# A long convolution and two split-precision MLPs on one core: the inverse transform of two tiles in one go, two PSUM buffers for `ob`, weight conversions every seven pairs, the last unit in halves

## The chip, the cores and the metric

One core of one Trainium2 chip runs the program. The metric is the device time of one execution in microseconds (us).

## The reference

```python
def _attn_ref(x, v, pos_emb, w1, w2):            # x, v: 1 x 12480 x 128
    h_filt = (np.maximum(pos_emb @ w1, 0) @ w2) * np.exp(-0.01 * np.arange(S))[:, None]
    u = x * v
    y = irfft(rfft(u, 2 * S) * rfft(h_filt, 2 * S))[:S]      # along the sequence
    return x * y
def _moe_ref(x, w_in, w_out):                    # 128 -> 2048 -> 128
    r = np.maximum(x @ w_in, 0); return (r * r) @ w_out
def _moe2_ref(x, w_in, w_out):
    h = x @ w_in; return (h / (1 + np.exp(-1.702 * h))) @ w_out
# result = _moe2_ref(_moe_ref(_attn_ref(...)))
```

The weights of the two MLPs are float64 in the reference's inputs, the rest is float32.

## The kernel before, in words

**Convolution.** The sequence is folded into N1 = 99 by N2 = 127, and the transform is done in two stages of matmuls in fp32. The stage `stage_s2` (from about 88 to 226 us) works through NP = 50 pairs of frequencies. In step p of its loop TensorE does `spectra(p)` (into `xk`), in odd steps also `features` (into `fk`), in every fourth step two `filters` (into `hk`), and then `back(p - 2)` (into `ob`). VectorE does `product(p - 1)` (four products `t` in one instruction, L374, and a difference into `P`, L378), GpSimd does the matching sum (L377), and ScalarE copies `fk`, `hk` and `ob` out of PSUM. `ob` goes to `A` (L390) and from there to the DRAM buffer `bd`. In PSUM `xk` and `hk` have two buffers each, `fk` one and `ob` one (pool `obp`).

**Weights.** The float64 weights are read as pairs of 32-bit words. `conversion` makes of each chunk a high and a low part in fp32r, in nine instructions: eight on VectorE (L149, L151, L155, L157, L158, L160, L165, L169) and a copy on ScalarE (L167). An object `Weights` starts chunks by a table (start, gap, lead); each `tick` lets every running conversion issue its next instruction. The eight chunks of the first MLP start at steps 3, 9, 15, ... of `stage_s2`, one tick for each pair; `work.finish` issues what is left before the MLP. The four chunks of the second MLP start at units 6, 18, 30 and 42 of the MLP loop.

**MLP loop.** The 12480 positions are cut into 25 tiles of 490 to 502 columns. A unit is a pair of 128-wide blocks of the 2048 hidden features of one tile: `unit_in` does six matmuls of about 500 columns into `hin` (three for each block: high times high, low times high, high times low), ScalarE and VectorE make `gh` and `gl` of it (`gate`, `high`, `low`), and `unit_out` does six matmuls into `acc`, LAG = 4 units later. Eight units make a tile. The first 40 units are all of the first MLP (layer 0); from then on units of both layers alternate. When tile `t`'s layer 0 is done, `split` makes the input of its layer 1.

**Inverse transform.** The convolution's last step lies inside that loop. `load_b` brings pieces of `bd` into `uv`, `combine_two` adds and subtracts them on VectorE into `b` (three homes, two of them in the old tile `Gs`), and `front_y(t + 1)` in unit j = 3 of tile t (4 from t = 5 on) does the inverse of one tile in TensorE: 5 segments with 4 small matmuls each (99x64 weights, 98 or 99 columns, fp32) into `yps`, which has two buffers in the pool `pms`. VectorE multiplies `yps` with x into `y` (L566), and `front_x` splits `y`. Two segments at the sequence's end are done by `front_rest` in unit j = 1 of tile 1, copied into `yr` (L587) and given out to the tiles from 2 on. Ahead of the loop the inverse of tile 0 stands between dummy matmuls (`spare`).

**Order.** Every engine runs its instructions in the order in which the code is written (`manual_schedule`). An instruction of an engine that waits holds up all that stand behind it there.

Of the kernel before, what the change touches and what calls it, by code (L numbers as in the profile page):

```python
# [23 lines left out]
N1, N2 = 99, 127  # L24
# [48 lines left out]
def widths():  # L73
# [25 lines left out]
def conv_mlp_kernel(ctx: ExitStack, tc: tile.TileContext, xc, xt, vc, pt, w1, w2,  # L99
# [76 lines left out]
    class Weights:  # L176
# [145 lines left out]
    def stage_s2(sp, mp, A, w2b, hooks, work):  # L322
# [3 lines left out]
        obp = tc.tile_pool(name="obp", bufs=1, space=PSUM, reuse_waits="tile")  # L326
# [5 lines left out]
        with kp as kp, obp as obp:  # L332
            def features(g):
# [5 lines left out]
                ps = kp.tile([128, FK, 128], FP32, tag="fk", name="fk", bufs=1)  # L339
# [98 lines left out]
    b_t, x_t, pending = {}, {}, []  # L438
# [29 lines left out]
    def pend(k):  # L468
        pending.extend((k, op) for op in (ALU.add, ALU.subtract))

    def combine_next(n):
        for i in range(min(n, len(pending))):
            combine_two(*pending.pop(0))

    def load_b(bp, t):


        last = max(p[0] for p in whole(t)) // JG
        for k in range(loaded[0], last + 1):
            uv = bp.tile([N1, 2, JG, 2, D], FP32, tag="uv", name="uv", bufs=2)  # L480
            for h in range(2):
                nc.sync.dma_start(out=uv[:, h], in_=bd[h, k * JG:(k + 1) * JG].rearrange("j k c d -> k j c d"))
            b = sums(bp, k % 3)
            b_t[k] = uv, b
            pend(k)
        loaded[0] = last + 1
# [23 lines left out]
    def mlp(lp, bp, work):  # L510
# [44 lines left out]

        def front_y(t):


            ps = pms.tile([D, 512], FP32, tag="m", name="yps")
            inverse(ps, whole(t))  # L560
            if t == 0:
                return split_first(ps, x_t.pop(0)[:, 0:width(0)])
# [9 lines left out]
        def load_rest():  # L572


            k = REST[0][0] // JG
            assert all(p[0] // JG == k for p in REST)
# [315 lines left out]
```

## Time and profile before

| | us |
|---|---|
| median of 3 runs (1381.61 to 1383.54) | 1382.43 |
| the profiled execution | 1382.61 |
| span of its instructions | 1380.8 |
| TensorE busy (matmuls) | 1372.9 (99%) |
| VectorE busy | 1109.2 (80%) |
| ScalarE busy | 948.9 (69%) |
| GpSimd busy | 61.0 (4%) |

The span runs from the first instruction to the last. The profiled execution is 1.8 us longer than its span. In a row of a timeline the first number is the start and the second the length, both in us; PE is TensorE's matmul stream, PEld its weight loads, DVE VectorE, ACT ScalarE. A matmul's recorded length overlaps that of the next, so the step from one start to the next tells what it takes of TensorE. An fp32 matmul stands in the trace as two records with a load each, and an fp32r matmul as one.

### The profile page before, as it was taken

Reading aid. Unit: us, or ns where it says so; the run is one execution under the profiler, and the core shown is the slowest. Engines: PE = TensorE matmul, PEld = TensorE weight load, DVE = VectorE, ACT = ScalarE, POOL = GpSimd, SP = SyncE. Lnnn points to the kernel's source line nnn. Section 1 sums busy time; section 2 is a strip of 40 time slices with the busy share of each in tenths; the row PEclk is TensorE's granted clock in tenths of the full one; section 3 lists DMA queues with packets and bytes.
Section 4 is the critical chain, followed back from the end, with each engine's and each line's share of the span. In section 5 each row is a group of like instructions: output and inputs, shape, how many; then the busy total and the mean of one; then the engine's idle time right before and its main releaser. Section 6 shows DMA issues by size and latency. Waiting matters only on the chain.

```text
span 1380.8 us, 19037 instructions
## 1 busy us (share of the span) xinstructions
PE 1372.9 (99%) x7754; PEld 1139.9 (83%) x7754; DVE 1109.2 (80%) x1224; ACT 948.9 (69%) x1066; POOL 61.0 (4%) x61
## 2 busy tenths in 40 slices
PE   9999999999999999999999999999999999999998
PEld 8888886888888888888888888888888888888887
DVE  7559998888887787778777887778777887778887
ACT  2655554888776777667767777777777777777776
POOL 3013332000000000000000000000000000000000
PEclk9999999999999999999999999999999999999999
DMA  9968875111210000000000100001000000000000
GB/s 257 306 214 271 270 263 190 55 48 61 70 39 20 15 21 27 20 28 20 27 20 8 40 27 20 8 28 39 20 15 20 28 19 8 9 8 8 9 15 15
DMA packets 45843, 89.25 MB, mean 65 GB/s; under 512 B 4135, under 2 KB 30556, under 8 KB 44988
## 3 DMA queue, kind: packets, MB, share of 16 engines
q1 hardware_dynamic: 36744, 63.33, 15.4%
q10 hardware_dynamic: 9012, 24.70, 4.7%
q8 instruction: 61, 1.00, 0.3%
q14 instruction: 26, 0.21, 0.0%
HBM read 63.21 MB, written 24.81 MB: 64 GB/s over the span
## 4 chain that ended last, share of the span: by engine, by line
PE 92%; DVE 6%; issue 1%; ACT 1%; DMA 1%; SPq 0%; DVEq 0%; ACTq 0%
PE acc L595 13%; PE acc L596 13%; PE acc L597 13%; PE hin L595 13%; PE hin L596 13%; PE hin L597 13%; PE s L295 5%; PE yps L553 3%; DVE t L374 2%; PE ob L388 2%; PE xk L365 2%; PE hk L357 1%; PE fk L342 1%; DVE r L278 1%; DVE words L151 0%
## 5 line engine op out<-in xcount | busy, mean ns | idle before, releaser
L647 DVE TENSOR_TENSOR gl<-g,gh 128x1004 fp32r<-128x1004 f32 (+4 forms) x400 | 477.1, 1193 | 36.9 <-ACT gh L643 36.8
L623 ACT ACTIVATE g<-hin 128x1004 f32<-128x1004 f32 (+4 forms) x200 | 201.0, 1005 | 225.3 <-PE hin L597 219.2
L595 PE MATMUL acc<-gh,w 128*128 128x502 f32 (+4 forms) x800 | 313.8, 392 | 0.6 <-DVE lo L530 0.6
L596 PE MATMUL acc<-gl,w 128*128 128x502 f32 (+4 forms) x800 | 311.4, 389 | 0.6 <-DVE gl L647 0.6
L597 PE MATMUL acc<-gh,w 128*128 128x502 f32 (+4 forms) x800 | 311.4, 389 | 0.0
L595 PE MATMUL hin<-hi,w 128*128 128x502 f32 (+4 forms) x798 | 310.3, 389 | 0.3 <-ACT g L623 0.3
L596 PE MATMUL hin<-lo,w 128*128 128x502 f32 (+4 forms) x798 | 310.5, 389 | 0.0
L597 PE MATMUL hin<-hi,w 128*128 128x502 f32 (+4 forms) x798 | 309.4, 388 | 0.0
L638 DVE TENSOR_TENSOR g<-hin,g 128x1004 f32<-128x1004 f32 (+4 forms) x200 | 238.7, 1194 | 45.7 <-ACT g L628 45.5
L628 ACT ACTIVATE g<-hin 128x1004 f32<-128x1004 f32 (+4 forms) x200 | 200.1, 1000 | 70.4 <-PE hin L597 62.4
L636 DVE CAST gh<-g 128x1004 fp32r<-128x1004 f32 (+4 forms) x185 | 125.8, 680 | 137.1 <-ACT g L624 137.0
L624 ACT ACTIVATE g<-g 128x1004 f32<-128x1004 f32 (+4 forms) x200 | 208.0, 1040 | 6.3
L643 ACT CAST gh<-g 128x1004 fp32r<-128x1004 f32 (+4 forms) x200 | 202.7, 1013 | 0.3 <-DVE g L638 0.3
L595 PEld LDWEIGHTS acc<-gh,w 128*128 128x128 f32 x800 | 150.5, 188 | 33.9 <-DVE lo L530 1.0
L595 PEld LDWEIGHTS hin<-hi,w 128*128 128x128 f32 x798 | 150.2, 188 | 34.1 <-ACT g L623 3.5
L596 PEld LDWEIGHTS acc<-gl,w 128*128 128x128 f32 x800 | 150.9, 189 | 30.4 <-DVE gl L647 1.4
L597 PEld LDWEIGHTS acc<-gh,w 128*128 128x128 f32 x800 | 150.5, 188 | 30.4
L597 PEld LDWEIGHTS hin<-hi,w 128*128 128x128 f32 x798 | 150.4, 188 | 30.4
L596 PEld LDWEIGHTS hin<-lo,w 128*128 128x128 f32 x798 | 150.3, 188 | 30.2
L374 DVE TENSOR_TENSOR t<-xk,hc 128x1024 f32<-128x1024 f32 (+1 forms) x50 | 60.1, 1202 | 11.6 <-ACT hc L359 11.6
L377 POOL TENSOR_TENSOR P<-t 128x256 f32<-128x256 f32 (+1 forms) x50 | 48.4, 968 | 155.4 <-DVE t L374 141.0
L388 PE MATMUL ob<-P,m 128*128 128x256 f32 x198 | 53.0, 391 | 0.3 <-issue 0.3
(79 smaller groups left out, 954.2 us busy)
## 6 DMA issues: line engine op xcount, KB each, us to landing
m<-in_c_s_dram SPq DMA_DIRECT2D x49, 256.0 KB
bd<-A ACTq DMA_DIRECT2D x24, 512.0 KB
uv<-bd SPq DMA_DIRECT2D x62, 198.0 KB
x<-in_xc_dram SPq DMA_DIRECT2D x16, 384.0 KB
v<-in_vc_dram SPq DMA_DIRECT2D x16, 384.0 KB
Gs<-gd ACTq DMA_DIRECT2D x10, 512.0 KB
gd<-G SPq DMA_DIRECT2D x3, 1344.0 KB
pos<-in_pt_dram SPq DMA_DIRECT2D x16, 198.0 KB
```

The lines of the kernel that those rows point to most:

```text
L374: nc.vector.tensor_tensor(out=t[:, 0:n], in0=xk[:, 0:n].unsqueeze(3).to_broadcast(full), in1=hc.unsqueeze(2).to_broadcast(full), op=ALU.mult)
L388: nc.tensor.matmul(out=ob[:, j], lhsT=m[:, j, 1, :], rhs=P[:, j])
L595: nc.tensor.matmul(out=out, lhsT=a, rhs=hl[0], start=first, stop=False)
L596: nc.tensor.matmul(out=out, lhsT=a, rhs=hl[1], start=False, stop=False)
L597: nc.tensor.matmul(out=out, lhsT=b, rhs=hl[0], start=False, stop=last)
L623: nc.scalar.activation(out=g, in_=ps, func=ACTF.Relu)
L624: nc.scalar.activation(out=g, in_=g, func=ACTF.Square)
L628: nc.scalar.activation(out=g, in_=ps, func=ACTF.Sigmoid, scale=1.702)
L636: nc.vector.tensor_copy(out=gh, in_=g)
L638: nc.vector.tensor_tensor(out=g, in0=ps, in1=g, op=ALU.mult)
L643: nc.scalar.copy(out=gh, in_=g)
L647: nc.vector.tensor_tensor(out=gl, in0=g, in1=gh.bitcast(FP32), op=ALU.subtract)
```

## The change

The kernel after does these things otherwise:

- `ob` and `fk` share one tag with two PSUM buffers, and the pool `obp` is gone.
- The first MLP's conversions start at steps 3, 10, 17, ... of `stage_s2` (gap 7 in place of 6, fetched 7 steps ahead). The eighth chunk does not start there, and the end of the seventh is left too; both are issued in the first seven units of the MLP loop, one or two ticks a unit (`rest.go_on`). The second MLP's chunks start at units 10, 21, 32 and 43.
- `front_ps` does the inverse of tiles t + 1 and t + 2 one behind the other, in even tiles t alone. `front_rest` stands in the same place of tile 2, ahead of the two. The first such place is unit 2. The products with x follow in that unit and the next (`front_y`).
- The pieces of `bd` come by a queue (`queue_for`, `load_next`, `combine_next`): at most two are loaded and not yet summed, and a sum is issued two or more steps of the loop behind its load. The four sums for tiles 1 and 2 stand ahead of the loop.
- In the last unit each 128-wide block has a PSUM tile, a sigmoid, a product, a cast and a difference of its own, and the last output is copied and sent in two halves of 245 columns, by two queues.

```diff
@@ widths
-        if t > 1 and left:
-            n = min(left, -(-RESTW // (NTILE - 2)))
+        if t > 2 and left:
+            n = min(left, -(-RESTW // (NTILE - 3)))
@@ Weights
-        def finish(self, n=1 << 30):
-            while n and (self.run or self.plan):
-                self.tick(1 << 30)
-                n -= 1
+        def go_on(self, n, at=0):
+            for i in range(n):
+                self.tick(at)
@@ stage_s2
-        obp = tc.tile_pool(name="obp", bufs=1, space=PSUM, reuse_waits="tile")
-                ps = kp.tile([128, FK, 128], FP32, tag="fk", name="fk", bufs=1)
+                ps = kp.tile([128, FK, 128], FP32, tag="fk", name="fk")
-                ob = (kp.tile([128, FK, D], FP32, tag="fk", name="ob", bufs=1).rearrange(
-                    "p (k c) d -> p k c d", c=2) if p == NP - 2 else
-                      obp.tile([128, 2, 2, D], FP32, tag="ob", name="ob"))
+                ob = kp.tile([128, FK, D], FP32, tag="fk", name="ob").rearrange("p (k c) d -> p k c d", c=2)
@@ loads and sums of the inverse
+    def load_sum(bp, k, n):
+        b_t[k] = load_uv(bp, k), home_of.pop(k)() if k in home_of else sums(bp, k % 3)
+        pending.extend((n, k, op) for op in (ALU.add, ALU.subtract))
+    def combine_next(n, most=1):
+        for i in range(most):
+            if pending and pending[0][0] <= n:
+                combine_two(*pending.pop(0)[1:])
+    def load_next(bp, n):
+        if queue and len({k for _, k, _ in pending}) < 2:
+            load_sum(bp, queue.pop(0), n + 2)
@@ the inverse
+        def front_ps(t):
+            ps_t[t] = pms.tile([D, 512], FP32, tag="m", name="yps")
+            inverse(ps_t[t], whole(t))
         def front_y(t):
-            ps = pms.tile([D, 512], FP32, tag="m", name="yps")
-            inverse(ps, whole(t))
+            ps = ps_t.pop(t)
@@ the last unit and the last output
+            if (l, t, j) == seq[-1]:
+                ps = ps[:, 0, 0:n], pms.tile([128, 512], FP32, tag="m", name="hin")[:, 0:n]
+            if (l, t, j) == seq[-1]:
+                for c in range(2):
+                    nc.scalar.activation(out=g[:, c], in_=ps[c], func=ACTF.Sigmoid, scale=1.702)
+            elif (l, t, j) == seq[-1]:
+                for c in range(2):
+                    nc.vector.tensor_tensor(out=g[:, c], in0=ps[c], in1=g[:, c], op=ALU.mult)
+                    cut = w // 2 if t == NTILE - 1 else w
+                    for a, b, queue in ((0, cut, nc.sync if cut < w else nc.scalar), (cut, w, nc.scalar)):
+                        if a < b:
+                            nc.scalar.copy(out=o[:, a:b], in_=acc[1][:, a:b])
+                            queue.dma_start(out=out[:, STARTS[t] + a:STARTS[t] + b], in_=o[:, a:b])
@@ ahead of the loop
-        front_y(0)
+        front_first()
-        work.finish()
+        queue_for(1)
+        queue_for(2)
+        load_next(bp, -2)
+        load_next(bp, -2)
+        load_x(lp, 1)
+        load_x(lp, 2)
+        combine_next(0, 4)
-        work = Weights([(2, 0), (3, 0), (2, 1), (3, 1)], 6, 12, 4)
+        rest, work = work, Weights([(2, 0), (3, 0), (2, 1), (3, 1)], 10, 10.67, 3)
@@ the loop
+            rest.go_on(1 if n < 2 else 2, 1 << 30)
-                    if t == 1 and j == 1:
-                        front_rest()
-                    if j == 3 + late and t + 1 < NTILE:
-                        front_y(t + 1)
+                    at = 3 + (t >= SHIFT // PAIRS) if t else 2
+                    lead = t % 2 == 0 and t + 2 < NTILE
+                    if lead and j == at:
+                        if t == 2:
+                            front_rest()
+                        front_ps(t + 1)
+                        front_ps(t + 2)
+                        front_y(t + 1)
+                    elif lead and j == at + 1:
+                        front_y(t + 2)
+                    load_next(bp, n)
@@ the call of stage_s2
-            work = Weights([(i, c) for c in range(NWC) for i in range(2)], 3, 6, 5)
+            work = Weights([(i, c) for c in range(NWC) for i in range(2)], 3, 7, 7)
-            work.finish(EARLY)
+            work.go_on(EARLY)
```

The change moves instructions at three places that matter below. The first is TensorE at the start of the MLP loop, where `hin` is a unit's first matmuls, `yps` an inverse and `acc` a unit's second matmuls. Before, from the fourth unit's last matmuls on, the inverse of tile 1 alone stands ahead of the first `acc`:

```order
L595 MATMUL hin<-hi_2304,w_958 128x492
L596 MATMUL hin<-lo_2305,w_958 128x492
L597 MATMUL hin<-hi_2304,w_958 128x492
L553 MATMUL yps<-ci_61,Gs 64x99 x8
L553 MATMUL yps<-ci_61,b 64x99 x4
L553 MATMUL yps<-ci_61,b 64x98 x4
L553 MATMUL yps<-ci_61,b 64x99 x4
L595 MATMUL acc<-gh,w_958 128x492
```

After, the inverse of tiles 1 and 2 stands behind the third unit, ahead of the fourth:

```order
L558 MATMUL yps<-ci_61,Gs 64x99 x8
L558 MATMUL yps<-ci_61,b 64x99 x4
L558 MATMUL yps<-ci_61,b 64x98 x4
L558 MATMUL yps<-ci_61,b 64x99 x4
L558 MATMUL yps<-ci_61,b 64x98 x4
L558 MATMUL yps<-ci_61,Gs 64x99 x4
L558 MATMUL yps<-ci_61,Gs 64x98 x4
L558 MATMUL yps<-ci_61,Gs 64x99 x4
L558 MATMUL yps<-ci_61,Gs 64x98 x4
L600 MATMUL hin<-hi_2291,w_958 128x492
```

So 40 small matmuls in place of 20 stand there, one unit earlier.

The second place is VectorE at the same time: `lo` is the last of tile 0's input, `uv` what the sums read, `gh` and `gl` the first unit's results. Before, a unit's work comes ahead of the sums:

```order
L543 TENSOR_TENSOR lo_2305<-y,hi_2304 128x492
L169 TENSOR_TENSOR w_958<-words,w_958 128x512
L636 CAST gh<-g 128x2x492
L647 TENSOR_TENSOR gl<-g,gh 128x2x492
L464 TENSOR_TENSOR b<-uv 99x2x256
L466 TENSOR_TENSOR b<-uv 99x2x2x128
```

After, four sums come first, and instructions of two conversions lie between the units':

```order
L548 TENSOR_TENSOR lo_2292<-y,hi_2291 128x492
L460 TENSOR_TENSOR b<-uv 99x2x256
L462 TENSOR_TENSOR b<-uv 99x2x2x128
L460 TENSOR_TENSOR Gs<-uv 99x2x256
L462 TENSOR_TENSOR Gs<-uv 99x2x2x128
L149 TENSOR_SCALAR words<-words 128x512
L653 CAST gh<-g 128x2x492
L169 TENSOR_TENSOR w_958<-words,w_958 128x512
L151 SCALAR_TENSOR_TENSOR words<-words 128x512
L669 TENSOR_TENSOR gl<-g,gh 128x2x492
```

The sums moved ahead of everything of the loop, and the eighth conversion moved in from `stage_s2`.

The third place is unit j = 3 of tile 2. Before, TensorE has the inverse of tile 3 there, and VectorE's row at that time ends in the product of tile 3 with x:

```order
L151 SCALAR_TENSOR_TENSOR words<-words 128x1024
L530 TENSOR_TENSOR lo_2792<-acc,hi_2791 128x494
L636 CAST gh<-g 128x1004
L647 TENSOR_TENSOR gl<-g,gh 128x1004
L566 TENSOR_TENSOR y<-yps,xs 128x493
```

After, TensorE has the rest's eight matmuls and the inverse of tiles 3 and 4, in three tiles of a pool with two buffers, so that the third takes the buffer of the rest:

```order
L558 MATMUL yps<-ci_61,words 64x98 x8
L558 MATMUL yps<-ci_61,Gs 64x99 x4
L558 MATMUL yps<-ci_61,Gs 64x98 x4
L558 MATMUL yps<-ci_61,Gs 64x99 x4
L558 MATMUL yps<-ci_61,Gs 64x98 x4
L558 MATMUL yps<-ci_61,b 64x99 x4
L558 MATMUL yps<-ci_61,b 64x98 x4
L558 MATMUL yps<-ci_61,b 64x99 x4
```

and VectorE, at the same time, has the rest's copy into `yr` where the product of tile 3 stood:

```order
L169 TENSOR_TENSOR w_2239<-words,w_2239 128x1024
L535 TENSOR_TENSOR lo_2782<-acc,hi_2781 128x494
L653 CAST gh<-g 128x2x492
L669 TENSOR_TENSOR gl<-g,gh 128x2x492
L592 COPY yr<-yps 128x196
L579 TENSOR_TENSOR y<-yps,xs 128x493
```

The second row with `b` in TensorE's piece is where tile 4 begins; its first matmul waits for VectorE.

## Rows read from the trace of the kernel before

**Rows 1.** The page, part 1: busy us (share) xinstructions of each engine.

```profile
PE 1372.9 (99%) x7754; PEld 1139.9 (83%) x7754; DVE 1109.2 (80%) x1224; ACT 948.9 (69%) x1066; POOL 61.0 (4%) x61
```

**Rows 2.** Waits from 88 to 227 us: us in total, times, longest.

```profile
PEld ob L388 <- issue: 3.4, 13, 0.7
PEld xk L365 <- DVE t L374: 2.8, 9, 0.6
```

**Rows 3.** Timeline, weight loads of `stage_s2`: start, length, instruction, idle before it.

```profile
100.23 1.86 PEld L357 LDWEIGHTS hk<-w2b,fs 64*128 64x128 f32 x32 [0.33 <-issue]
...
155.65 1.86 PEld L357 LDWEIGHTS hk<-w2b,fs 64*128 64x128 f32 x32 [0.33 <-issue]
...
162.08 0.73 PEld L388 LDWEIGHTS ob<-P,m 128*128 128x128 f32 x4 [0.23 <-issue]
...
166.62 1.86 PEld L357 LDWEIGHTS hk<-w2b,fs 64*128 64x128 f32 x32 [0.33 <-issue]
...
211.56 1.86 PEld L357 LDWEIGHTS hk<-w2b,fs 64*128 64x128 f32 x32 [0.33 <-issue]
```

**Rows 4.** Timeline, VectorE in `stage_s2` and at its end.

```profile
199.29 1.22 DVE L165 SCALAR_TENSOR_TENSOR words<-words 128x512 f32<-128x512 f32 x1
...
216.22 1.22 DVE L165 SCALAR_TENSOR_TENSOR words<-words 128x512 f32<-128x512 f32 x1
...
219.36 1.22 DVE L374 TENSOR_TENSOR t<-xk,hc 128x1024 f32<-128x1024 f32 x1
...
221.03 1.22 DVE L374 TENSOR_TENSOR t<-xk,hc 128x1024 f32<-128x1024 f32 x1
```

**Rows 5.** The tile `yps`: idle time of the loader before its loads (us, times).

```profile
  issue: 8.8, 25
```

**Rows 6.** Timeline, TensorE around the inverse of tile 6.

```profile
376.58 0.39 PE L597 MATMUL hin<-hi,w 128*128 128x502 f32 x1
376.90 0.56 PE L553 MATMUL yps<-ci,Gs 99*64 99x98 f32 x8
377.29 1.53 PE L553 MATMUL yps<-ci,b 99*64 99x99 f32 x32
378.75 0.49 PE L595 MATMUL acc<-gh,w 128*128 128x492 f32 x1
379.07 0.39 PE L596 MATMUL acc<-gl,w 128*128 128x492 f32 x1
```

**Rows 7.** Timeline, start of the MLP loop.

```profile
236.31 0.67 DVE L543 TENSOR_TENSOR lo<-y,hi 128x492 fp32r<-128x492 f32 x1
...
240.06 0.38 PE L597 MATMUL hin<-hi,w 128*128 128x492 f32 x1
240.77 0.49 PE L595 MATMUL hin<-hi,w 128*128 128x492 f32 x1 [0.33 <-ACT g L623]
...
244.20 0.49 PE L595 MATMUL acc<-gh,w 128*128 128x492 f32 x1
```

**Rows 8.** Timeline: the rest's copy, and tile 3's inverse and product.

```profile
264.24 0.35 DVE L587 COPY yr<-yps 128x196 f32<-128x196 f32 x1
...
290.71 0.48 PE L553 MATMUL yps<-ci,Gs 99*64 99x99 f32 x6
...
295.56 0.66 DVE L566 TENSOR_TENSOR y<-yps,xs 128x493 f32<-128x493 f32 x1
```

**Rows 9.** Windows: length, busy us of PE, PEld, DVE, ACT, POOL; PEclk; DMA; GB/s.

```profile
266.00:290.00 24.00, 24.00 (x139) 19.71 (x138) 20.15 (x25) 20.73 (x23) 0.00 (x0) 1.00 0.26 83
...
1379.00:1380.80 1.80, 0.00 (x0) 0.00 (x0) 0.00 (x0) 0.00 (x0) 0.00 (x0) 0.59 0.13 47
```

**Rows 10.** Timeline, TensorE where the layers begin to alternate.

```profile
365.87 0.49 PE L595 MATMUL acc<-gh,w 128*128 128x492 f32 x1 [0.61 <-DVE lo L530]
```

**Rows 11.** Timeline, the end.

```profile
1374.40 0.49 PE L596 MATMUL acc<-gl,w 128*128 128x490 f32 x1 [0.56 <-DVE gl L647]
...
1377.13 0.57 ACT L666 COPY o<-acc 128x490 f32<-128x490 f32 x1 [2.83 <-PE acc L597]
```

More of the change, by code (lines that the diff above doesn't have):

```diff
@@ L330, in pair @@
             return min(2, N1 - 2 * p)
-        with kp as kp, obp as obp:
+        with kp as kp:
             def features(g):
@@ L466, in combine_two, with load_uv, queue_for @@
             nc.vector.tensor_tensor(out=b[:, :, 0:4:3], in0=u, in1=v[:, :, ::-1], op=op)
[L468 to L475, printed above, removed]
-        last = max(p[0] for p in whole(t)) // JG
[L479 to L486, printed above, removed]
+    def load_uv(bp, k):
+        uv = bp.tile([N1, 2, JG, 2, D], FP32, tag="uv", name="uv", bufs=2)
+        for h in range(2):
+            nc.sync.dma_start(out=uv[:, h], in_=bd[h, k * JG:(k + 1) * JG].rearrange("j k c d -> k j c d"))
+        return uv
+    def load_sum(bp, k, n):
+        b_t[k] = load_uv(bp, k), home_of.pop(k)() if k in home_of else sums(bp, k % 3)
+        pending.extend((n, k, op) for op in (ALU.add, ALU.subtract))
+    def queue_for(t):
+        last = max(p[0] for p in whole(t)) // JG
+        queue.extend(range(loaded[0], last + 1))
+        loaded[0] = max(loaded[0], last + 1)
+    def combine_next(n, most=1):
[5 more added lines that the diff above has]
+            load_sum(bp, queue.pop(0), n + 2)
     late_h = []
@@ L570, in front_y, with rest_home @@
             y_t[t] = y
-        def load_rest():
-            k = REST[0][0] // JG
-            assert all(p[0] // JG == k for p in REST)
-            uv = bp.tile([N1, 2, JG, 2, D], FP32, tag="uv", name="uv", bufs=2)
-            for h in range(2):
-                nc.sync.dma_start(out=uv[:, h], in_=bd[h, k * JG:(k + 1) * JG].rearrange("j k c d -> k j c d"))
-            b = words(6, 2)[0:N1].bitcast(FP32).rearrange("p (j s c d) -> p j s c d", j=JG, s=2, c=2)
-            b_t[k] = uv, b
-            pend(k)
+        def rest_home():
+            return words(6, 2)[0:N1].bitcast(FP32).rearrange("p (j s c d) -> p j s c d", j=JG, s=2, c=2)
         def front_rest():
@@ L636, in gate @@
                 nc.vector.tensor_copy(out=gh, in_=g)
+            elif (l, t, j) == seq[-1]:
+                for c in range(2):
+                    nc.vector.tensor_tensor(out=g[:, c], in0=ps[c], in1=g[:, c], op=ALU.mult)
             else:
@@ L642, in high @@
             if l == 1:
-                nc.scalar.copy(out=gh, in_=g)
+                for c in halves((l, t, j)):
+                    nc.scalar.copy(out=gh[:, c], in_=g[:, c])
         def low(un):
             key, ps, g, gh, gl = un
-            nc.vector.tensor_tensor(out=gl, in0=g, in1=gh.bitcast(FP32), op=ALU.subtract)
+            for c in halves(key):
+                nc.vector.tensor_tensor(out=gl[:, c], in0=g[:, c], in1=gh.bitcast(FP32)[:, c], op=ALU.subtract)
             g_t[key] = (gh, gl)
@@ L664, in unit_out @@
                 else:
[L665 to L667 removed]
+                    o = tp.tile([D, MW], FP32, tag="o", name="o")
+                    w = width(t)
+                    cut = w // 2 if t == NTILE - 1 else w
[3 more added lines that the diff above has]
+                            queue.dma_start(out=out[:, STARTS[t] + a:STARTS[t] + b], in_=o[:, a:b])
         seq = []
@@ L683, in mlp @@
         spare(7)
-        front_y(0)
+        front_first()
         spare(1)
-        work.finish()
+        assert all(p[0] // JG == REST[0][0] // JG for p in REST)
+        home_of[REST[0][0] // JG] = rest_home
+        queue_for(1)
[5 more added lines that the diff above has]
+        combine_next(0, 4)
         prev = None
-        work = Weights([(2, 0), (3, 0), (2, 1), (3, 1)], 6, 12, 4)
+        rest, work = work, Weights([(2, 0), (3, 0), (2, 1), (3, 1)], 10, 10.67, 3)
         for n in range(len(seq) + LAG):
+            rest.go_on(1 if n < 2 else 2, 1 << 30)
             work.tick(n)
+            assert n < 7 or not rest.run and not rest.plan
             if n >= LAG:
```

45 lines of the change are left out of this document (24 added, 21 removed).

## The prediction

> **What bounds the kernel now.** I began with the page's busy shares: TensorE is busy for 1372.9 us of a span of 1380.8 [rows 1], so nothing that merely frees another engine can move the time; only TensorE's own small losses can. Then I looked for those losses. The list of waits over `stage_s2` names two: before `ob` the loader stood 3.4 us in 13 places, and before `xk` it waited 2.8 us in 9 places for VectorE's product `t` [rows 2]. The tile view of the inverse names a third: 25 times the loader sat idle before `yps`, 8.8 us in all, 0.35 us each [rows 5]. Since recorded matmuls overlap, I read the true price of such a place from the steps between starts [rows 6]. The timelines of the loop's start [rows 7], of the turn to alternating layers [rows 10] and of the end [rows 11] show one wait each. Together that is some 14 us that a change could reach, about 1% of the time. The rest of TensorE's time is matmuls back to back, which the change leaves in number and nearly in shape.
>
> **Part 1, two buffers for `ob` and conversions every seven pairs.** A period of four pairs ends with `hk`. An undisturbed one lasts 166.62 - 155.65 = 10.97 us and has one wait of 0.23 us before `ob` in it, at 162.08, where `ob` stands one step behind the previous `ob` and must wait for ScalarE to empty the one buffer [rows 3]. With two buffers shared with `fk`, that `ob` takes the buffer of a `fk` that was copied well before, so a period of pure work is 10.97 - 0.23 = 10.74 us. The ten periods from 100.23 to 211.56 took 111.33 us [rows 3], against 107.4 of pure work: 3.9 us are there to be won. But VectorE was the second limit, and it must allow that. Six pairs and one conversion take 216.22 - 199.29 = 16.93 us on it, and a bare pair 221.03 - 219.36 = 1.67 us [rows 4], so a conversion is 16.93 - 6 x 1.67 = 6.91 us. Before, that is 2.82 us a pair, more than TensorE's 10.74 / 4 = 2.69; this is where the waits for `t` come from. After, it is (7 x 1.67 + 6.91) / 7 = 2.66 us a pair, just under 2.69. TensorE becomes the bound, with 1% to spare. The spare is thin and the work is uneven: with a gap of seven, two conversion instructions fall into one pair of every seven, so that VectorE falls behind for a step. I leave 0.7 us of the waits for `t` in, and take 3.2 us off. At the stage's end the same wait for `ob` delays the last pairs; the chain there runs on through the copy, `bd` and the first inverse, and I take 0.3 us more. Part 1: **-3.5 us**, bounds -4.4 (all waits gone, and 0.5 at the end) and -1.5 (VectorE keeps most of its waits). The conversion that leaves the stage goes to the MLP's first units, where VectorE's row has it between the units' work; its cover there is the four units that lie between a unit's first and second matmuls.
>
> **Part 2, the inverse of two tiles in one go.** From 376.58 to 379.07 TensorE goes from a long matmul over one inverse to the second long matmul behind it: 2.49 us [rows 6]. Two long steps in their own place cost 2 x 0.23 = 0.46. The small records are 0.0415 us apart: the last of the 32 starts at 377.29 + 1.53 - 0.25 = 378.57, so (378.57 - 377.29) / 31. Forty of them are 1.70 with their slower first ones. What is left, 2.49 - 0.46 - 1.70 = 0.33 us, is paid for each change of shape, out and back, whatever stands between. There are 25 such places [rows 5]: 24 tiles and the rest. After, 12 are left. Part 2: 13 x 0.33 = **-4.3 us**, bounds -3.9 and -4.5.
>
> **Part 3, a new wait in tile 2.** There the rest and two tiles take three tiles of PSUM from a pool with two buffers. Tile 4's inverse takes the buffer of the rest, so it waits until VectorE has copied the rest into `yr`. VectorE's row there is the same as before up to that copy, with L169 in place of L151, one long conversion instruction for another. Before, its next instruction at this point, the product, began at 295.56, and the inverse had begun at 290.71 [rows 8]. The copy takes 0.35 [rows 8], so the buffer is free at 295.91, or 5.2 us after the inverse's start. TensorE has the rest's 16 records and tile 3's 40 to do until then, 56 x 0.043 = 2.4 us. It then stands for 5.2 - 2.4 = **+2.8 us**, and behind it in TensorE's row stand `acc` and all the rest of the program, so nothing hides it. Bounds: +2.0, if ScalarE and VectorE take up the unit without delay, and +3.4, if ScalarE is still busy with the unit before it.
>
> **Part 4, the loop's start.** Before, the fourth unit's matmuls waited for ScalarE to empty `hin`: the step from 240.06 to 240.77 is 0.71 where 0.23 is usual [rows 7]. After, two inverses fill that hole: **-0.5 us**. The cover needs four sums to be ready. They stand directly behind `lo`, which ends at 236.98 [rows 7]; at 0.6 each, about the step of `lo`-sized instructions, they would end near 239.4, and the inverse could start at 240.4. Their last one is needed only half way through, near 242. If the transfers of `uv` come 2.6 us later than I think, the gain is gone, and each us more costs one. Bounds -0.6 and +1.0.
>
> **Part 5, the rest.** Where layers begin to alternate, `acc` waited 0.61 us for `lo`, held up by a long conversion instruction [rows 10]. After, a short one stands there, but also a sum, and tile 5's inverse no longer gives VectorE a rest: -0.2 us, bounds -0.5 and +0.5. At the end TensorE waited 0.56 us for the last `gl` but one [rows 11]; with the sigmoid and the product in halves that begins about 0.3 us earlier. Of the 0.57 us of the last copy [rows 11], half comes ahead of the first transfer, which may save 0.2. Together **-0.5**, bounds -0.8 and -0.1. The waits that stand on SyncE's queue (the loads of x and `uv` for two tiles) are issued a tile ahead of their use; I cost them at nothing, covered by those 16 units.
>
> **Sum.** -3.5 - 4.3 + 2.8 - 0.5 - 0.2 - 0.5 = -6.2 us. The profiled execution took 1382.6, its span and 1.8 around it, and stands 0.2 above the median of the runs, 1382.43, which is less than I can resolve. Summed against 1382.6 that gives **1376.4 us**.
>
> **Rivals.**
>
> *A. The clock falls in the new wait.* At the end of the program, when TensorE has done nothing since the last `acc`, the granted clock of the last 1.8 us is 0.59 on average [rows 9], so it falls from 2.4 to 1.2 GHz after an idle stretch. The new wait of 2.8 us is longer than any other that TensorE has inside the loop. If the clock falls there, TensorE works at half speed until it is granted again; no row prices that, and 6 us at half speed, 3 us lost, is my choice between 0 and 10. Time 1379.4. Against it: the wait is not as long as the idle stretch at the end, and dense work stands on both sides. The Trainium skill, "TensorE: Matmul & The Clock Gate", section "HAM oscillation — how this bites in real kernels", tells that waits between groups of matmuls send the engine back to the lower clock, each anew. By that rule this case would be likelier than I put it; the trace of before has no such wait within the loop to show it.
>
> *B. VectorE keeps `stage_s2`.* With 2.66 us against 2.69 a pair there is hardly any room, and GpSimd works at the same time. If VectorE stays the bound at uneven pairs, part 1 gives 1.5 and the time is 1378.4.
>
> *C. The new wait isn't there or is short,* because VectorE gets to the copy earlier or the wait takes the place of one that would come behind it. The time is 1373.6. For it: units behind a long break find everything ready. Against it: before, TensorE shows no waits in that stretch to be saved.
>
> *D. Slower: the first layer runs out of cover.* For the first 40 units ScalarE and VectorE do nearly as much as TensorE: 20.73 and 20.15 us in 24.0 [rows 9], of which one inverse gave TensorE's partners 2.0 us of rest in every tile. In odd tiles that rest is gone, and 20.73 of 22.0 us is 94%. If the chain through ScalarE, VectorE and back gets longer than the four units' lag, every unit waits. It decides from 22.0 us of ScalarE's work in a tile on, 1.3 us more than now. To end above 1385.2 it would have to cost 9 us over four tiles, 0.28 us in each of 32 units; then 1386. Against it: before, ScalarE is idle at the end of each tile, and no `acc` waits there.
>
> **How the numbers follow.** Forecast 0.53, A 0.17, B 0.12, C 0.12, D 0.06. The range takes in B and A on one side and C on the other: 1373.5 to 1380.2. A measurement of this kernel tells about 0.2% or 2.8 us from no change, so faster means under 1379.7. The forecast, C, B and nearly half of A lie there: 0.83. The other half of A and what lies between forecast and D: 0.12. D alone makes it slower: 0.05.
>
> **What would show it.** In the trace after: no idle before `ob` in steps with an even pair, and periods of `hk` of 10.74 to 10.85 us; 12 places with idle time before `yps` in place of 25 beside tile 0's; one wait of TensorE for `yr` of 2 to 3.4 us near 290; no idle between the third and fourth unit; a first wait for `gl` at the end under 0.4 us. The forecast is wrong if the clock after 290 us is under 1.00, if the waits before `xk` stay at nearly 3 us, if TensorE waits for sums at unit 2, or if `acc` waits for `gl` in tiles 1 to 4.

## The result, and the profile after

The changed kernel takes 1389.62 us (median of four runs, 1389.27 to 1390.99), the kernel before 1382.02 beside it: a ratio of 1.0055, 95% interval 1.0037 to 1.0072. It is slower by about 7.6 us. I had forecast 1376.4 us and a range up to 1380.2.

The page's busy shares of the changed kernel say no more than those of before [rows 1] did: TensorE has 1.2 us less work in a span that is 7.2 us longer.

```profile
PE 1371.7 (99%) x7754; PEld 1143.2 (82%) x7754; DVE 1108.6 (80%) x1226; ACT 948.4 (68%) x1069; POOL 61.0 (4%) x61
```

So the time lies in waits. The list of TensorE's waits (engine, tile, line, what it waited for: us in total, times, longest) is the view that tells it:

```profile
PE yps L558 <- DVE yr L592: 3.2, 1, 3.2
PE acc L602 <- DVE w L169: 2.6, 1, 2.6
PE acc L601 <- DVE gl L669: 1.7, 3, 1.0
...
PE hin L600 <- ACT g L636: 0.9, 1, 0.9
PE acc L600 <- DVE lo L535: 0.7, 1, 0.7
```

The first was forecast. The second, the fourth and most of the third were not. To see where they stand in time, I read from the timeline when the first `hk`, the first `yps` and the first `acc` matmul of certain units start (a8 is unit 8's), and when the last instruction ends. The lengths between these points, in us, for the profiled execution of each kernel that was run:

| kernel | to first hk | to first yps | to a0 | to a8 | to a28 | to a56 | to the end |
|---|---|---|---|---|---|---|---|
| before | 91.08 | 141.50 | 11.62 | 24.50 | 58.82 | 81.11 | 972.19 |
| after | 90.63 | 139.22 | 12.80 | 24.37 | 63.90 | 87.80 | 969.24 |
| e1_gap | 90.08 | 138.79 | 12.77 | 24.08 | 64.89 | 85.19 | 969.13 |
| e2_rest | 90.06 | 139.81 | 12.78 | 24.86 | 58.16 | 87.79 | 969.18 |
| e4_start | 90.63 | 138.84 | 12.77 | 21.46 | 63.92 | 86.35 | 969.16 |
| e5_ob | 90.57 | 141.17 | 11.56 | 24.51 | 58.80 | 81.13 | 972.21 |
| e6_three | 91.13 | 140.61 | 12.73 | 22.36 | 58.12 | 84.08 | 969.13 |
| e7_split | 90.49 | 139.11 | 13.00 | 22.48 | 58.25 | 84.14 | 972.36 |
| e8_fill | 90.42 | 138.81 | 12.81 | 23.97 | 62.38 | 86.28 | 969.19 |
| e9_late | 91.19 | 140.01 | 12.76 | 22.35 | 58.13 | 82.91 | 969.19 |
| e10_six | 91.16 | 141.70 | 12.69 | 22.35 | 58.15 | 84.11 | 969.14 |

At a28, a56 and the end before and after have the same inverses behind them. Between the first `yps` and a8 they haven't: after, tile 2's inverse stands before a0 and not between a0 and a8, and the rest's stands behind a8. Four things can be read from the two first lines, beside the way to the first `hk`, which differs by up to 1.1 us between kernels that are alike there. The stage before the loop gained 2.3 us. The loop's start, which has fewer inverses in it now, is hardly shorter. Between a8 and a56 some 11.8 us were lost. And from a56 on 2.95 us were gained, where the forecast puts 3.5 (nine places and the end).

In the stage itself a period of four pairs (weight loads of `hk`: start, length, instruction, idle before it) is now 10.88 us, with one exception in ten (165.03 and 175.91 are one period apart, 175.91 and 187.41 are the exception), where an undisturbed one was 10.97 before [rows 3]:

```profile
99.78 1.86 PEld L355 LDWEIGHTS hk<-w2b,fs 64*128 64x128 f32 x32 [0.33 <-issue]
...
165.03 1.86 PEld L355 LDWEIGHTS hk<-w2b,fs 64*128 64x128 f32 x32 [0.33 <-issue]
175.91 1.86 PEld L355 LDWEIGHTS hk<-w2b,fs 64*128 64x128 f32 x32 [0.33 <-issue]
187.41 1.86 PEld L355 LDWEIGHTS hk<-w2b,fs 64*128 64x128 f32 x32 [0.33 <-issue]
...
209.16 1.86 PEld L355 LDWEIGHTS hk<-w2b,fs 64*128 64x128 f32 x32 [0.33 <-issue]
```

At the loop's start ScalarE (first two lines, its idle time before them) and TensorE (the third and fourth) show a wait in a chain. The copy of the eighth conversion, L167, was put into ScalarE's row ahead of unit 4's relu. It waits for VectorE's L165, which stands behind two products in VectorE's own full row. ScalarE idles 3.90 us, and then the units' matmuls wait for their relu and their `gl`:

```profile
248.80 0.62 ACT L167 CAST w<-words 128x512 fp32r<-128x512 f32 x1 [3.90 <-DVE words L165]
249.33 0.98 ACT L636 ACTIVATE g<-hin 128x984 f32<-128x984 f32 x1
...
250.36 0.49 PE L600 MATMUL hin<-hi,w 128*128 128x492 f32 x1 [0.86 <-ACT g L636]
...
256.22 0.49 PE L601 MATMUL acc<-gl,w 128*128 128x492 f32 x1 [1.02 <-DVE gl L669]
```

At 294.71 stands the wait for `yr`. It is 3.23 us long, and behind it the steps between long matmuls are 0.41 us instead of 0.23 up to 299.65: there TensorE runs at the lower of its two clock levels, 1.2 GHz. The window (columns as in rows 9) gives a granted clock of 0.84 over these eleven us:

```profile
294.71 1.24 PE L558 MATMUL yps<-ci,b 99*64 99x98 f32 x24 [3.23 <-DVE yr L592]
295.78 0.91 PE L558 MATMUL yps<-ci,Gs 99*64 99x99 f32 x16
...
298.42 0.61 PE L601 MATMUL acc<-gl,w 128*128 128x492 f32 x1
298.83 0.61 PE L602 MATMUL acc<-gh,w 128*128 128x492 f32 x1
...
289.00:300.00 11.00, 7.77 (x105) 6.82 (x106) 9.12 (x14) 2.58 (x4) 0.00 (x0) 0.84 0.34 97
```

And up to 398.60 TensorE waited for a weight. VectorE's row shows why: L169, the last instruction of the second layer's fourth conversion, came only at 397.33, behind the products and differences of the units ahead of it.

```profile
396.21 1.19 DVE L669 TENSOR_TENSOR gl<-g,gh 128x1004 fp32r<-128x1004 f32 x1
397.33 1.22 DVE L169 TENSOR_TENSOR w<-words,w 128x1024 fp32r<-128x1024 f32 x1
...
398.60 0.59 PE L602 MATMUL acc<-gh,w 128*128 128x492 f32 x1 [2.64 <-DVE w L169]
398.98 0.61 PE L600 MATMUL acc<-gh,w 128*128 128x492 f32 x1
399.40 0.61 PE L601 MATMUL acc<-gl,w 128*128 128x492 f32 x1
```

The conversions of the second layer now begin at units 10 + 10.67 k. For the fourth, k = 3, that is 42.01, and a start in unit 43; before it was 6 + 12 x 3 = 42. So L169 stands in unit 52's row, and unit 49's second matmuls, which come in loop step 53, need its result. Behind this wait the clock fell again (steps of 0.41).

My theory from here on: three waits and two falls of the clock, all made by where single instructions stand in rows that are worked off in order, ate a gain that is otherwise there. The rival: VectorE has too little time throughout the first layer, and a wait that is mended comes back at the next row.

### The profile page after: what moved, and what is told of

Read it like the earlier page. It is cut to its first block, busy times and chain, and to the rows that moved or that the text cites. A ratio compares the mean times of both kernels' runs of the same rounds, so it can differ in the third digit from the quotient of the medians.

```text
span 1388.0 us, 19040 instructions
## 1 busy us (share of the span) xinstructions
PE 1371.7 (99%) x7754; PEld 1143.2 (82%) x7754; DVE 1108.6 (80%) x1226; ACT 948.4 (68%) x1069; POOL 61.0 (4%) x61
## 4 chain that ended last, share of the span: by engine, by line
PE 89%; DVE 7%; ACT 2%; DMA 1%; issue 1%; ACTq 0%; SPq 0%; DVEq 0%
PE acc L601 12%; PE acc L600 12%; PE acc L602 12%; PE hin L601 12%; PE hin L600 12%; PE hin L602 12%; PE s L294 5%; PE ob L384 3%; PE xk L363 3%; PE yps L558 3%; DVE gl L669 2%; PE hk L355 2%; PE fk L340 2%; DVE r L277 1%; ACT g L636 1%
## 5 line engine op out<-in xcount | busy, mean ns | idle before, releaser
L669 DVE TENSOR_TENSOR gl<-g,gh 128x1004 fp32r<-128x1004 f32 (+5 forms) x401 | 476.8, 1190 | 35.2 <-ACT gh L664 35.1
L653 DVE CAST gh<-g 128x1000 fp32r<-128x1000 f32 (+4 forms) x185 | 125.7, 680 | 134.4 <-ACT g L637 134.4
L664 ACT CAST gh<-g 128x1004 fp32r<-128x1004 f32 (+5 forms) x201 | 202.7, 1009 | 0.2 <-DVE g L658 0.2
```

Of the source, the lines that this page charges most:

```text
L653: nc.vector.tensor_copy(out=gh, in_=g)
L664: nc.scalar.copy(out=gh[:, c], in_=g[:, c])
L669: nc.vector.tensor_tensor(out=gl[:, c], in0=g[:, c], in1=gh.bitcast(FP32)[:, c], op=ALU.subtract)
```

## The experiments

Where lengths are given, they are from the table above. All but e5_ob are edits of the changed kernel, or of e6_three where the text says so.

**e1_gap: the fourth conversion one unit earlier.**

```diff
-Weights([(2, 0), (3, 0), (2, 1), (3, 1)], 10, 10.67, 3)
+Weights([(2, 0), (3, 0), (2, 1), (3, 1)], 10, 10.66, 3)
```

> The changed kernel with 10.66 for 10.67 as the distance of the second layer's conversions, so that the fourth starts in unit 42, as it did before, and not in 43; nothing else. Theory (one late instruction): TensorE's 2.6 us wait for w behind L169 at 395.9 us goes, and with it the fall of the granted clock behind it (0.86 in 396:400, about 1.7 us more), so 4.3 to 5 us less than the changed kernel's 1389.6: 1384.6 to 1385.3, and no wait of an acc matmul for w. Rival (VectorE has too much to do in units 42 to 52, 100% busy at 365 to 392 us): the work only moves one unit ahead, the same time is lost as waits for gl, and at most 1 us is gained: 1388.6 or more.

Measured: 1386.65 us, 3.0 less than the changed kernel; ratio to before 1.0033 (1.0020 to 1.0046). The wait for w is gone. But a28 to a56 became only 2.6 us shorter, since L149 and L151 now stand one unit earlier too, and L151 stands ahead of `lo`:

```profile
371.60 1.22 DVE L151 SCALAR_TENSOR_TENSOR words<-words 128x1024 f32<-128x1024 uint32 x1
372.73 0.67 DVE L535 TENSOR_TENSOR lo<-acc,hi 128x502 fp32r<-128x502 f32 x1
...
373.46 0.49 PE L600 MATMUL acc<-gh,w 128*128 128x492 f32 x1 [1.84 <-DVE lo L535]
```

TensorE waits 1.84 us for `lo`, where the changed kernel waited 0.70, and the clock fell behind it (steps of 0.41 from 374.08 to 376.95). In the kernel before, L151 stood ahead of `lo` too and that wait was 0.61 us [rows 10]; what is new in VectorE's row there is a sum (L460, at 369.31). So the late instruction did cost its 2.64 us, but the rival has a part in it: that stretch of VectorE's row is full. The 3.0 us are less than the 4.3 that I expected for another reason as well: in this execution the lower clock behind the wait for `yr` lasted longer (granted clock 0.69 from 289 to 300 us, where the changed kernel had 0.84), and a8 to a28 became 1.0 us longer.

**e2_rest: the rest's inverse out of tile 2's group.**

```diff
                     if lead and j == at:
-                        if t == 2:
-                            front_rest()
                         front_ps(t + 1)
...
+                    if t == 1 and j == 3:
+                        front_rest()
```

> The changed kernel with the inverse of the pooled rest (front_rest) taken out of the group of tile 2 and put back into tile 1, behind its fourth pair, where the kernel before had it next to its second; nothing else. Theory: the wait of yps for yr (3.2 us at 294.7 us) goes, the granted clock stays at 1.00 there (it was 0.84 in 289:300, about 1.6 us), and one more change of tile shape is paid (0.33 us): about 4.5 us less than 1389.6, so 1385.1. Rival (the wait only takes the place of time that VectorE needs anyway for the two tiles' products and sums): the wait turns up at the next gl, and under 1.5 us is gained: 1388 or more.

Measured: 1383.84 us, 5.8 less than the changed kernel; ratio to before 1.0011 (1.0001 to 1.0020). The wait for `yr` is gone, and a8 to a28 is 5.74 us shorter. The inverse of the rest itself moved ahead of a8; it takes 0.9 us (e6_three beside e4_start), which leaves 4.8 for the wait and the clock behind it, about what I expected. The rival fails here: no later row took the time up.

**e4_start: the end of the eighth conversion spread out.**

```diff
-            rest.go_on(1 if n < 2 else 2, 1 << 30)
+            rest.go_on((1, 1, 2, 2, 1, 0, 2, 1, 1)[n] if n < 9 else 0, 1 << 30)
```

> The changed kernel with the eighth conversion's last three instructions later: its product (L165) alone in loop step 4, nothing in step 5, ScalarE's copy (L167) in step 6 and not 4, VectorE's low part (L169) in step 7; nothing else. Theory (ScalarE's row in order): the copy no longer stands ahead of unit 4's relu waiting for VectorE (3.9 us of idle time on ScalarE before 248.80 us), the waits for g and gl at 250 to 256 us go, and the way from the first acc matmul (a0) to the ninth (a8) is some 1.9 us shorter than the changed kernel's 24.37 us: 1387.7. Rival (VectorE is what is late there, with 100% busy time from 239 to 251 us): the waits stay, now for gl alone, and under 0.7 us is gained.

Measured: 1386.42 us, 3.2 less; ratio to before 1.0030 (1.0020 to 1.0039). a0 to a8 is 2.91 us shorter, more than the two waits that I had counted, 0.86 and 1.02. The steps between starts tell why: the step with a listed wait in it and the step behind it together cost about 0.27 us more than the list gives, 1.1 and 1.3 us for these two, and a third stop, too short for the list (0.06), cost 0.3. L167 now runs without a wait, and TensorE has none between 241 and 266 us:

```profile
250.57 0.62 ACT L167 CAST w<-words 128x512 fp32r<-128x512 f32 x1
```

In this execution TensorE waited 2.7 us for w as the changed kernel did, but the clock did not fall behind that wait (1.00 in the window), and a28 to a56 is 1.45 us shorter for it:

```profile
386.00:396.00 10.00, 6.73 (x30) 5.03 (x29) 8.88 (x10) 8.26 (x9) 0.00 (x0) 1.00 0.01 2
```

**e8_fill: the wait for `yr` filled with matmuls that nobody reads.** They stand between the inverse of tile 3 and that of tile 4, where the wait is, and not ahead of both as the expectation has it. The run separates the wait from the clock.

```diff
+        def fill(n):
+            ps = pac.tile([128, MW], FP32, tag="acc", name="spare")
+            for i in range(n):
+                nc.tensor.matmul(out=ps[:, 0:width(2)], lhsT=wts[0][:, 0, 0:128], rhs=xin[0][2][0])
...
                         front_ps(t + 1)
+                        if t == 2:
+                            fill(14)
                         front_ps(t + 2)
```

> The changed kernel with 14 matmuls of 128 x 128 x 494 that nobody reads, between the rest's inverse and the two tiles' inverse, where TensorE waits 3.2 us for yr. Theory (the fall of the granted clock behind that wait comes from TensorE standing still): the inverse starts at the same time, 3.1 to 3.4 us of idle time are filled, the granted clock is 1.00 in the ten us behind it, and 1.7 us are gained: 1387.9. Rival (the clock falls for another reason, or the matmuls delay the inverse by more than they save): the row of 289 to 300 us still has a granted clock of 0.7 to 0.9, and the time is 1389 or more.

Measured: 1387.50 us, 2.1 less; ratio to before 1.0035 (1.0021 to 1.0048). The second inverse starts no sooner (27.7 us behind a8 in both kernels), but the clock stays:

```profile
290.39 3.35 PE L711 MATMUL spare<-hi,w 128*128 128x492 f32 x14
293.69 1.24 PE L558 MATMUL yps<-ci,b 99*64 99x98 f32 x24
...
295.86 0.39 PE L601 MATMUL acc<-gl,w 128*128 128x492 f32 x1
296.09 0.39 PE L602 MATMUL acc<-gh,w 128*128 128x492 f32 x1
...
289.00:300.00 11.00, 11.00 (x110) 9.32 (x105) 8.33 (x13) 3.00 (x4) 0.00 (x0) 1.00 0.23 67
```

The steps of `acc` are 0.23 again, and a8 to a28 is 62.38 in place of 63.90. So this fall of the clock costs 1.5 us, and it comes from TensorE standing still.

**e5_ob: the two buffers alone, in the kernel before.**

```diff
-                ob = (kp.tile([128, FK, D], FP32, tag="fk", name="ob", bufs=1).rearrange(
-                    "p (k c) d -> p k c d", c=2) if p == NP - 2 else
-                      obp.tile([128, 2, 2, D], FP32, tag="ob", name="ob"))
+                ob = kp.tile([128, FK, D], FP32, tag="fk", name="ob").rearrange("p (k c) d -> p k c d", c=2)
```

> The kernel before with one edit of the change alone: ob takes turns in the two buffers of fk and has no pool of its own; the conversions stay at every six pairs and end ahead of the sums, the loop is untouched. Theory (the prediction's part 1, two halves): the waits for ob (3.4 us in 13) go, but VectorE with a conversion every six pairs stays the pace in part of the stage, so the first inverse starts 0.5 to 1.5 us earlier than the 232.58 us of before: 1381.0 to 1381.9. Rival (the buffer is all of it): the first inverse starts 2.7 us earlier, as in the changed kernel (229.85 us): 1379.7.

Measured: 1382.51 us; ratio to before 1.0001 (0.9991 to 1.0010). The waits for `ob` on the buffer are gone from the list of 88 to 227 us, and those for `t` have grown from 2.8 us [rows 2] to:

```profile
PEld xk L364 <- DVE t L373: 3.8, 10, 0.7
```

The first `hk` to the first inverse is 0.33 us shorter, less than the 0.5 to 1.5 that I expected. By itself the buffer turns one wait into another; the rival, that it is all of the gain, fails.

**e6_three: all three places mended.** e2_rest and e4_start together, and in place of e1_gap:

```diff
-            work.tick(n)
+            work.go_on(2 if n == 50 else 1, n)
```

> The changed kernel with three of its moves mended together: front_rest in tile 1 as in e2_rest; the eighth conversion's end spread as in e4_start; and the fourth conversion of the second layer still beginning in unit 43, but with two ticks in step 50, so that its last instruction (L169) stands in VectorE's row one unit earlier, as before the change, while nothing is put ahead of lo at 372 us as e1_gap did. Theory (the changed kernel lost its gain in these three places and the rest of the sum holds): by the times of the acc matmuls, 2.9 us less between a0 and a8 (24.37 to 21.46 in e4_start), 5.7 less between a8 and a28 (63.90 to 58.16 in e2_rest), 4.4 less between a48 and a52 (15.28, and 10.83 in e1_gap), together 13.1 from 1389.6: 1376.5, faster than the kernel before by 0.4%. Rival (VectorE is short of time through the whole first layer, and each mended wait comes back at the next row, as 1.1 of 1.8 us did at lo in e1_gap): 1379 to 1382.

Measured: 1378.20 us (six runs, 1377.07 to 1379.94); ratio to before 0.9968 (0.9956 to 0.9980). That is 11.4 us less than the changed kernel and 0.3% faster than before. My 13.1 had counted the rest's inverse in neither stretch, 0.9 us, and a48 to a52 kept a wait for w, listed with 0.4, that made it 0.7 us longer than in e1_gap. What is left for TensorE in the loop:

```profile
PE acc L600 <- DVE lo L535: 0.7, 1, 0.7
PE acc L601 <- DVE gl L669: 0.7, 2, 0.4
...
PE hin L600 <- DVE g L658: 0.6, 1, 0.6
...
PE acc L602 <- DVE w L169: 0.4, 1, 0.4
```

These lie between a28 and a56, which still takes 2.97 us more than before.

**e9_late: two sums out of that stretch, on top of e6_three.**

```diff
-                if l == 0:
+                if l == 0 and not 41 <= n <= 52:
                     combine_next(n)
```

> e6_three with no sums on VectorE in steps 41 to 52: two instructions (L460 and L462 of the last group of columns fetched for tiles 7 and 8, 0.68 us each), which stood in the row beside the second layer's fourth conversion, move behind it, where the next inverse (step 65) still finds them done; nothing else. In e6_three the way from a28 to a56 is 84.08 us, 2.97 more than in the kernel before with the same inverses in it. Theory (what is left of the loss there is VectorE's row in order: two tiles' sums beside a conversion): the waits of TensorE for lo, g, gl and w at 372 to 398 us, 2.1 us together, fall to 0.8 or less and a28 to a56 is 1.0 to 1.5 us shorter: 1376.7 to 1377.2. Rival (the loss lies elsewhere, as in the change of the order of inverse and units): the waits shrink and come back at other rows, a28 to a56 within 0.3 us of 84.08: 1378.2.

Measured: 1376.90 us (1376.01 to 1378.32); ratio to before 0.9959 (0.9945 to 0.9972). a28 to a56 is 82.91, 1.17 us less, and the waits for `lo` and `g` have left the list:

```profile
PE acc L601 <- DVE gl L669: 0.7, 2, 0.4
...
PE acc L602 <- DVE w L169: 0.5, 1, 0.5
```

So the rival was right about this one stretch: two tiles' sums and a long conversion met there on VectorE. 1.8 us over the kernel before are left between a28 and a56. The two lines above are 1.2 us of waits there, where the kernel before had 0.6 [rows 10]. The rest shows in the steps between TensorE's starts. A listed wait of 0.37 makes the step that it lies in 0.76 us long and the step behind it 0.32, instead of 0.23 each, so it costs 0.6:

```profile
361.93 0.38 PE L600 MATMUL acc<-gh,w 128*128 128x502 f32 x1
362.69 0.49 PE L601 MATMUL acc<-gl,w 128*128 128x502 f32 x1 [0.37 <-DVE gl L669]
363.01 0.39 PE L602 MATMUL acc<-gh,w 128*128 128x502 f32 x1
```

Counted in this way TensorE stops seven times between a28 and a56 and loses 3.0 us; the kernel before stopped once, for `lo`, and lost 0.9. With the one place less that e9_late has there, 0.3 us, this makes the 1.8.

**e7_split: the inverses apart again, on top of e6_three.**

```diff
                         front_ps(t + 1)
-                        front_ps(t + 2)
                         front_y(t + 1)
...
                     elif lead and j == at + 1:
+                        front_ps(t + 2)
                         front_y(t + 2)
```

> e6_three with the inverse of two tiles taken apart again: the second tile's inverse stands one unit later, ahead of its own product, so that there are 25 groups of inverses in the loop and not 13; nothing else. Theory (the prediction's part 2: each group costs a change of tile shape of 0.33 us before and behind it): 12 more groups, 4.0 to 5.1 us more (0.33 to 0.42 us each) than e6_three, spread evenly over the tiles to the end. Rival (the merge brings little by itself and the gain between a64 and a399 came from elsewhere, such as fewer waits): under 1.5 us more.

Measured: 1381.63 us, 3.4 more than e6_three; ratio to before 0.9995 (0.9987 to 1.0004). From the first `yps` to the end it is 3.81 more, 0.32 for each of the 12 places (one of them lies ahead of a0), a little under the range that I gave. Two inverses in one go (the last `hin`, the inverses, the first `acc`) in e6_three:

```profile
513.07 0.38 PE L602 MATMUL hin<-hi,w 128*128 128x502 f32 x1
513.38 0.90 PE L558 MATMUL yps<-ci,b 99*64 99x99 f32 x16
514.12 2.89 PE L558 MATMUL yps<-ci,Gs 99*64 99x99 f32 x64
516.94 0.49 PE L600 MATMUL acc<-gh,w 128*128 128x502 f32 x1
517.27 0.39 PE L601 MATMUL acc<-gl,w 128*128 128x502 f32 x1
```

and apart in e7_split:

```profile
511.87 0.38 PE L602 MATMUL hin<-hi,w 128*128 128x502 f32 x1
512.18 0.90 PE L558 MATMUL yps<-ci,b 99*64 99x99 f32 x16
512.91 1.19 PE L558 MATMUL yps<-ci,Gs 99*64 99x99 f32 x24
514.04 0.50 PE L600 MATMUL acc<-gh,w 128*128 128x502 f32 x1
```

From `hin` to `acc` it is 3.87 us for two together and 2.17 for one. Twice 2.17 is 0.47 more; 0.23 of it is a long step of its own, and the step behind an inverse is 0.33 in place of 0.23, so a place costs 0.34 by these rows.

**e10_six: the first layer's conversions every six pairs again, on top of e6_three.**

```diff
-            work = Weights([(i, c) for c in range(NWC) for i in range(2)], 3, 7, 7)
+            work = Weights([(i, c) for c in range(NWC) for i in range(2)], 3, 6, 5)
```

> e6_three with the first layer's conversions at every six pairs again, fetched five pairs ahead, as before the change, so that they end in the second stage and ahead of the loop; ob keeps its two buffers; nothing else. Theory (the prediction's part 1: the two deferred ends take 0.16 us a pair off VectorE, which paces the stage): the first inverse starts 1.5 to 2 us later, counted from the first hk matmul (139.3 us in the mean of the seven kernels with conversions every seven pairs, 141.2 in e5_ob), the loop's start is at most 0.7 us shorter, and the time is 0.8 to 2 us more than e6_three's 1378.2: 1379.0 to 1380.2. Rival (the deferral only moves the work to the loop's start): no later than e6_three by a0 to a8 taken together: 1377.5 to 1378.4.

Measured: 1380.29 us, 2.1 more than e6_three, just over the range that I gave; ratio to before 0.9985 (0.9977 to 0.9994). The first `hk` to the first inverse is 141.70, 2.3 us more than the mean of the eight kernels with a distance of seven, 139.4, and more than each of them (138.8 to 140.6); the loop's start is no shorter (22.35), so once e4_start's order is used the deferred work costs nothing there. The rival fails.

## Why the prediction was wrong

**Part 1, right in direction, too large.** I put -3.5 us on it. From the first `hk` to the first inverse 2.3 us were won in the changed kernel, 2.1 in the mean of the eight kernels that have this part. The mis-sized step is the period of pure work. I subtracted the whole idle time before `ob` from the period; it became 10.88, so only 0.09 of the 0.23 were time. The loader's rows show where the rest was. Before, the step from `xk` to the `ob` that waits, at 162.08 [rows 3], was 1.07 us and the step behind it 0.76:

```profile
161.01 0.84 PEld L365 LDWEIGHTS xk<-A,m 128*128 128x128 f32 x4
...
162.84 0.84 PEld L365 LDWEIGHTS xk<-A,m 128*128 128x128 f32 x4
```

After, both are 0.86, so that half of the wait had been made up right behind it:

```profile
159.52 0.84 PEld L363 LDWEIGHTS xk<-A,m 128*128 128x128 f32 x4
160.38 0.84 PEld L384 LDWEIGHTS ob<-P,m 128*128 128x128 f32 x4
161.24 0.84 PEld L363 LDWEIGHTS xk<-A,m 128*128 128x128 f32 x4
```

The ten periods went from 111.33 [rows 3] to 109.39 us, where I had 108.1; the 0.3 us at the stage's end came. e5_ob and e10_six show that the buffer alone is not enough, as the limit of VectorE, 2.82 us a pair, had said. The distance of seven without the buffer was not run; by the undisturbed periods, 10.97 and 10.88, an estimate is that ten periods would then be at least 0.9 us longer than with both. Rival B (VectorE keeps the stage) did not come true. In the same stretch its waits for `t` fell from 2.8 us [rows 2] to:

```profile
PEld xk L363 <- DVE t L372: 0.6, 1, 0.6
```

**Part 1's last sentence, wrong.** "Its cover there is the four units that lie between a unit's first and second matmuls" named VectorE's row and forgot that a conversion also has a copy on ScalarE. That copy waits for VectorE and holds the relu that stands behind it. It cost 2.9 us (e4_start), and no term of the sum was there for it.

**Part 2, right.** The loader's idle time before `yps` fell from 25 places [rows 5] to 12. I had 0.33 us for each of 13; 12 of them measured 0.32, or 3.8 us (e7_split), which is 4.1 for 13. Not all of it shows from a56 on: nine places and 0.45 at the end would be 3.3 to 3.5 us, and 2.95 were measured, in part since the new widths move ten columns from tile 2 (492 in place of 502) to tiles 22 and 23 (500 and 492 in place of 492 and 490). A step of 502 columns is about 0.004 us longer than one of 492, which makes some 0.4 us over the 96 matmuls of a tile's layer, an estimate; so much moved from a8 to a28 to the stretch behind a56.

**Part 3, right about the wait, wrong about what follows it.** 3.23 us lie within the bounds of 2.0 to 3.4. But the sum took the wait alone and put the clock behind it at nothing; that was 1.5 us more (e8_fill).

**Part 4 and the end, right.** From the first `yps` to a0 it takes 1.18 us more with 1.70 us more of inverse in it: -0.52, where I had -0.5. From the start of the last `hin` matmul to the end it takes 9.79 us in place of 10.24: -0.45, where I had -0.5.

**Part 5's turn, the step that failed most.** I put -0.2 on the place where the layers begin to alternate, bounds -0.5 and +0.5, from a comparison of what stands ahead of `lo`. a28 to a56 became 6.69 us longer. I looked at the row where the kernel before waited, and not at the other end of the moved conversion: where its last instruction lands and who needs it. 42.01 in place of 42 is a whole unit, and TensorE needed that weight. It cost 2.6 us and a fall of the clock of 1.5. The two tiles' sums that now meet the conversion there cost another 1.2 (e9_late), and most of the rest are the short stops on VectorE that e9_late still has.

**Rival A, the clock: its chance was underrated, its price overrated.** I gave it 0.17 and 3 us. It fell behind the wait for `yr` in each of the three profiles that have this wait unfilled (after, e1_gap, e4_start), and cost 1.5 us in the changed kernel (e8_fill) and 2.5 in e1_gap; it fell behind the wait for w in two of four. The Trainium skill, "TensorE: Matmul & The Clock Gate", section "HAM oscillation — how this bites in real kernels", tells of waits between groups of matmuls that, where long enough, send the engine back, each anew. The traces agree for most waits and not for all: in e4_start and e8_fill waits of 2.7 and 2.6 us left the clock at 1.00.

**Rivals C and D.** C (the wait isn't there) fell. D was the only case on the slower side, and the time came out on its side, but not by its mechanism: no unit-by-unit loss shows from a8 to a28, the units of tiles 1 and 2 and half of tile 3: without the wait it is 58.16 (e2_rest), where before it was 58.82, with one place more and 0.4 us of wider matmuls. Its sign, a wait of `acc` for `gl`, shows once in tile 3 with 0.25 us (at 334.30).

Put together, from the two first lines of the table: -0.45 to the first `hk`, -2.28 to the first `yps`, +1.05 to a8, +5.08 to a28, +6.69 to a56, -2.95 to the end, which is 7.14 us. With the three places mended and the sums moved, e9_late stands at 1376.9. That this is near the forecast of 1376.4 is in part luck: e9_late has no wait for `yr`, and without the +2.8, with 0.33 for one place more, the prediction's terms give 1373.9. The 3 us above that are mainly part 1, which gave 2.1 in place of 3.5, and a28 to a56, which is still 1.8 longer than before. So the gain is there, at the size of some 5.5 us, and the places named above are what ate it.

## What to carry to other kernels

When a change sets the place of work by a formula, work out in which row each of its last instructions lands, on every engine it uses, and who needs the result. An instruction that waits holds everything behind it on its engine, so a deferred step is paid for by what stands behind it in that row. A listed wait of the matmul engine can cost more than its idle time: read the steps between starts on both sides of it. And a wait as long as the ones here, 1.84 to 3.25 us, should be priced with the clock behind it.

## What the runs showed of the hardware

Of eight waits of TensorE between 1.8 and 3.3 us inside the loop, seen in the profiles of after, e1_gap, e2_rest, e4_start and e8_fill, six were followed by matmuls at the lower clock, and two (2.7 and 2.6 us) were not. The shortest that was followed by it was 1.84 us (e1_gap). A fall cost 1.5 us by two ways of reading: 63.90 - 62.38 between a8 and a28 (e8_fill), and 87.80 - 86.35 between a28 and a56 (e4_start, where the same wait went by without it). It can cost more: in e1_gap the lower clock behind the wait for `yr` held longer, and 64.89 - 62.38 is 2.5 us. Kernels with such waits scatter with the clock that they are granted: the ten runs of e4_start lie between 1382.86 us (mean clock 1.000) and 1388.32 (0.996), those of e10_six, which has none, between 1379.57 and 1381.09.
